# Last two parts of the output: one transfer of 128 partitions each, one on SyncE's and one on ScalarE's queue

## Chip, core and metric

The kernel runs on one core of one Trainium2 chip. The metric is the device time of one execution in microseconds (us). Before the change the median of three runs is 298.77 us (298.04 to 298.97).

## What is computed

Retention attention without softmax, followed by a feed-forward block. The reference, cut to its arithmetic:

```python
# q, k, v: (B, H, S, D) = (8, 8, 576, 64), float32
scores = (1 / sqrt(D)) * q @ k.transpose(0, 1, 3, 2)
gamma = 1.0 - 2.0 ** (-5.0 - arange(H))
Dmat = where(rel >= 0, gamma[:, None, None] ** rel, 0.0)   # rel = position of query - position of key
attn = (scores * Dmat) @ v
x = attn.transpose(0, 2, 1, 3).reshape(4608, 512)
h = x @ w_in                  # w_in: (512, 2048)
g = h * cos(h)
out = g @ w_out               # w_out: (2048, 512); out: (4608, 512) float32
```

## The kernel before

The 4608 tokens are worked through in nine tiles of W = 512 tokens (`NT` = 9, `last` = 8). Attention runs in blocks of 256 tokens ahead of them and leaves `xT`, the bf16 operand of the first matrix product. For each tile, `mm1` (matmuls at line 506) gives `h`, ScalarE gives the cosine (line 519) and VectorE multiplies the two into `gT` (line 522). The second product is `mm2_seven`: the product of a 512-token tile with `w_out` is cut into two by two quarters and made from seven block products instead of eight, numbered 1, 2, 6, 4, 7, 5, 3 in the order in which they run. Each block product covers 256 tokens by `N2` = 256 output columns and 1024 inner elements. The sums of quarters of `gT` that it needs are made at line 565, its matmuls stand in `product` (line 626), ScalarE copies results out of PSUM into `ot` tiles (line 656), and VectorE adds the rest (line 652). The order of the work on every engine is written out by hand; the tile framework adds the semaphore waits that the data need.

A tile of 256 tokens is two groups `j` of P = 128 rows. Within a group, the partition p holds the row 2 * i + r of the group, with r = p // 64 and i = p % 64 (HP = 64): partitions 0 to 63 hold the even rows and partitions 64 to 127 the odd rows. `stored_rows` (line 636; the issues are at line 642) therefore writes a tile by two DMAs of 64 partitions, one for each r, given to the two queues in `queues`:

```python
rows = out[r0 : r0 + P * t.shape[1], c0:c1].rearrange(
    "(j i r) c -> r i j c", r=2, i=HP
)
for r in range(2):
    queues[r].dma_start(rows[r], t[r * HP : (r + 1) * HP])
```

Elsewhere in the kernel both queues are SyncE's; in the last tile, all stores but the first go by one DMA on SyncE's and one on ScalarE's queue.

The place of the change is the very end of the last tile. There the block products 5 and 3 have three parts instead of two, set in `product`:

```python
if x in (5, 3) and n == last:
    parts = [(0, 0, N2), (1, 0, N2 // 2), (1, N2 // 2, N2)]
```

Each part is a group j and a range of columns: 128 rows by 256 columns, then twice 128 rows by 128 columns. Product 3 runs part after part. In the last branch of `mm2_seven`, each part is added to `u1` by VectorE and stored at once, so that the first part's store goes out while TensorE works on the next part.

Of the kernel before, what the change touches and what calls it, by code (L numbers as in the profile page):

```python
# [17 lines left out]
def kernel(  # L18
# [9 lines left out]
    nc = tc.nc  # L28
    P = 128
# [13 lines left out]
    N2 = DM // 2  # L43

    W = 512
# [47 lines left out]
    tiles = {}  # L93
# [496 lines left out]
    def late_sums(n, xs):  # L590
        for x in xs:
            g_sum(n, x, 6 if x == 5 and n > 1 else 0 if x == 3 and n == 2 else 4, E2)
# [43 lines left out]
    def stored_rows(r0, c0, c1, t, queues=(nc.sync, nc.sync)):  # L636
# [7 lines that stand above are left out]
    def mm2_seven(n, at, stored, xs=(1, 2, 6, 4, 7, 5, 3), halfway=None):  # L644
        pend = []

        def flush():
            while pend:
                pend.pop(0)()

        def add(out_, in0, in1):
            return lambda: nc.vector.tensor_tensor(out=out_, in0=in0, in1=in1, op=ALU.add)  # L652

        def copied(tag, x):
            t = op.tile([P, 2, N2], F32, tag=tag, name="ot")
            held.append(lambda ps=tiles["all", x]: nc.scalar.copy(t, ps))  # L656
            return t

        def store(t, r, c, s):
            def go():  # L660
                queues = (nc.sync, nc.scalar) if n == last and s else (nc.sync, nc.sync)
                stored_rows(n * W + r * 256, c * N2, (c + 1) * N2, t, queues)
                stored(s)

            return go

        def copies():
            while held:
                held.pop(0)()

        for x in xs:
            if x not in at:
                copies()
                flush()
            else:
                if at[x].__name__ in ("nothing", "first_scores", "last_outputs", "only_intro", "turning"):
                    copies()
                at[x](flush, pend)
                copies()
            if x == 6 and n > 1:  # L680
                late_sums(n, (3,))
            parts = product(n, x, halfway)
            if x == 1:
                c11 = copied("a", 1)
                tiles["c11"] = c11
                if n > 1:
                    late_sums(n, (5, 6))
            elif x == 2:
                c11 = tiles["c11"]
                if n == 1:  # L690
                    p2 = copied("d", 2)
                    continue
                pend[:0] = [add(c11, c11, tiles["all", 2]), store(c11, 0, 0, 0)]
            elif x == 6:
                u1 = copied("b", 1)
            elif x == 4:
                c21 = copied("c", 4)
            elif x == 7 and n == 1:
                pend += [
                    add(c21, c21, tiles["all", 1]),  # L700
                    add(c22, c22, tiles["all", 1]),
                    store(c21, 1, 0, 1),
                    store(c22, 1, 1, 2),
                    add(c11, c11, p2),
                    store(c11, 0, 0, 0),
                ]
            elif x == 7:
                c22 = copied("d", 1)
                pend += [add(c21, c21, tiles["all", 1]), store(c21, 1, 0, 1)]
            elif x == 5 and n == 1:  # L710
                c22 = copied("d", 5)
            elif x == 5 and n == last:
                for (j, c0, c1), ps in zip(parts, tiles["o", 5]):
                    pend.append(add(c22[:, j, c0:c1], ps, c22[:, j, c0:c1]))
                pend.append(store(c22, 1, 1, 2))
            elif x == 5:
                pend += [
                    add(c22, c22, tiles["all", 5]),
                    add(u1, u1, tiles["all", 5]),
                    store(c22, 1, 1, 2),  # L720
                ]
            elif n < last:
                pend += [add(u1, u1, tiles["all", 5 if n == 1 else 3]), store(u1, 0, 1, 3)]
                flush()
            else:
                flush()
                copies()
                for (j, c0, c1), ps in zip(parts, tiles["o", 5]):
                    add(u1[:, j, c0:c1], ps, u1[:, j, c0:c1])()
                    stored_rows(  # L730
                        n * W + j * P, N2 + c0, N2 + c1, u1[:, j : j + 1, c0:c1],
                        (nc.sync, nc.scalar),
                    )

    loaded, prepared = 2, 0

# [204 lines left out]
    for n in range(NT):  # L941
        blocks = blocks_of.get(n) or [(e + k * E2, 0, W) for e in range(0, E2, 2) for k in range(2)]
        for i, (et, c0, cw) in enumerate(blocks):
# [25 lines left out]
            if (n, i) == (1, 3):  # L969
                mm2_seven(1, {}, None, (1,), lambda: (outputs(3, "m"), off.pop()()))  # L970
# [133 lines left out]
        def stored(u):  # L1104
            if n == 1:
                if u == 0:
                    step(False)
            else:
                steps_to({0: 2 * n + 6, 3: 2 * n + 7}.get(u, 0))

        mm2_seven(n, at, stored, *([(2, 4, 6, 5, 7, 3)] if n == 1 else []))


# [28 lines left out]
```

## Time and profile before

| | |
|---|---|
| median of the runs | 298.77 us (298.04, 298.97, 298.77) |
| profiled execution | 298.03 us |
| its span, first to last instruction | 296.3 us |
| TensorE matmuls busy | 284.4 us, 96% of the span |
| TensorE weight loads busy | 195.9 us, 66% |
| VectorE busy | 215.7 us, 73% |
| ScalarE busy | 170.2 us, 57% |
| GpSimd busy | 141.1 us, 48% |
| granted TensorE clock | 0.997 |
| read from and written to HBM | 36.70 MB and 9.44 MB |

In the profile's names PE is TensorE's matmuls, PEld its weight loads, DVE is VectorE, ACT is ScalarE, POOL is GpSimd and SP is SyncE; a q behind the name (SPq, ACTq) is the engine's sequencer, which among other things issues DMAs. L642 is line 642 of the kernel. Busy shares are averages over the whole span; the chain of waits tells which engine's work the end waited for. An issue's duration is the time for which it holds its queue; the data move later, and the landing is the time from the start of the issue to the last completion.

### The profile page before, as it was taken

What the parts mean: (1) busy time and instruction counts of PE and PEld (TensorE: products, weight loads), DVE (VectorE), ACT (ScalarE), POOL (GpSimd) and SP (SyncE); (2) the same over time, 40 slices, a digit from 0 to 9 for tenths busy, and PEclk for the clock granted to TensorE, in tenths of its full rate; (3) what the DMA queues carried; (4) which work ended last, traced back from release to release, by engine and by line L of the source; (5) the groups of instructions that cost most, each with busy time, mean ns of one, the idle gap of its engine ahead of it and who ended that gap; (6) DMA issues with size and microseconds to landing.
All of it is one profiled execution on the core that took longest, in us unless ns stands there. A gap on an engine that the chain in (4) does not pass through costs nothing.

```text
span 296.3 us, 10512 instructions
## 1 busy us (share of the span) xinstructions
PE 284.4 (96%) x4366; PEld 195.9 (66%) x4386; DVE 215.7 (73%) x307; ACT 170.2 (57%) x200; POOL 141.1 (48%) x162
## 2 busy tenths in 40 slices
PE   7989999889999999999999999999999999999994
PEld 2568545768864687458845884588458845884584
DVE  5756747859947887698769866986698669745943
ACT  4856316467458844767476747684668466535620
POOL 7621454961495995349424952495149013101400
PEclk9999999999999999999999999999999999999998
DMA  7999999988979958833965289429201220112013
GB/s 224 282 207 220 243 242 219 251 217 218 235 177 226 233 122 189 205 83 79 226 156 115 60 211 215 91 48 260 57 0 40 53 57 0 40 44 65 0 38 106
DMA packets 103981, 42.62 MB, mean 144 GB/s; under 512 B 68480, under 2 KB 103424, under 8 KB 103936
## 3 DMA queue, kind: packets, MB, share of 16 engines
q1 hardware_dynamic: 99184, 37.37, 52.0%
q0 software_dynamic: 4224, 4.19, 8.5%
q8 instruction: 36, 0.59, 0.9%
q10 hardware_dynamic: 528, 0.39, 0.4%
q14 instruction: 9, 0.07, 0.1%
HBM read 36.70 MB, written 9.44 MB: 156 GB/s over the span
## 4 chain that ended last, share of the span: by engine, by line
PE 84%; DMA 5%; DVE 4%; ACT 3%; issue 1%; POOL 1%; SPq 1%; ACTq 0%; POOLq 0%
PE h L506 39%; PE o L626 32%; PE o L1012 4%; DMA w_in_sb<-in_moe_w_in_dram 3%; PE tr L238 3%; PE ov L436 2%; DMA fk<-in_k_dram 2%; PE ov L463 1%; PE st L351 1%; PE sc L318 1%; ACT qkT L244 1%; DVE ret L327 1%; DVE gT L522 1%; SPq L139 1%; POOL qks L202 1%
## 5 line engine op out<-in xcount | busy, mean ns | idle before, releaser
L506 PE MATMUL h<-xT,w_in_sb 128*128 128x512 bf16 (+1 forms) x689 | 126.9, 340 | 1.4 <-DVE gT L522 0.2
L522 DVE TENSOR_TENSOR gT<-h,cosh 128x1024 bf16<-128x1024 f32 x72 | 87.6, 1221 | 32.1 <-ACT cosh L519 31.7
L506 PEld LDWEIGHTS <-w_in_sb 128*128 128x128 bf16 x704 | 68.0, 98 | 55.6 <-DMA w_in_sb<-in_moe_w_in_dram 0.7
L519 ACT ACTIVATE cosh<-h,half_pi 128x1024 f32<-128x1024 f32 x72 | 79.9, 1114 | 39.2 <-PE h L506 39.2
L565 POOL TENSOR_TENSOR gs<-gT 128x512 bf16<-128x512 bf16 x28 | 35.8, 1278 | 100.5 <-DVE gT L522 100.3
L626 PEld LDWEIGHTS <-gs 128*128 128x128 bf16 x528 | 49.6, 98 | 6.0
L626 PEld LDWEIGHTS <-gT 128*128 128x128 bf16 x384 | 36.6, 98 | 6.1
L202 POOL TENSOR_TENSOR qks<-fk,gkc 128x512 bf16<-128x512 f32 x32 | 37.6, 1193 | 5.1 <-DMA fk<-in_k_dram 5.1
L652 DVE TENSOR_TENSOR ot<-ot,o 128x512 f32<-128x512 f32 x35 | 23.2, 683 | 22.9 <-ACT ot L656 12.1
L202 POOL TENSOR_TENSOR qks<-fq,gq 128x512 bf16<-128x512 f32 x29 | 32.2, 1129 | 9.8 <-DMA fq<-in_q_dram 9.6
L244 ACT COPY qkT<-tr 128x1024 bf16<-128x1024 bf16 x28 | 26.8, 1021 | 9.9 <-PE tr L238 9.9
L410 ACT CAST sb<-s_all 128x768 bf16<-128x768 f32 (+2 forms) x18 | 16.3, 904 | 25.4 <-DVE s_all L400 21.1
L626 PE MATMUL o<-w_out_sb,gs 128*128 128x256 bf16 (+1 forms) x264 | 30.6, 270 | 0.1
L626 PE MATMUL o<-w_out_sb,gT 128*128 128x256 bf16 x256 | 30.6, 273 | 0.0
L626 PE MATMUL o<-ws,gs 128*128 128x256 bf16 (+1 forms) x264 | 30.4, 269 | 0.0
L656 ACT COPY ot<-o 128x512 f32<-128x512 f32 x33 | 19.2, 583 | 16.1 <-PE o L626 16.1
L327 DVE TENSOR_TENSOR ret<-sc,mask_c 128x512 bf16<-128x512 f32 x32 | 20.7, 684 | 5.9 <-PE sc L318 4.0
L213 POOL CAST vb<-fv 128x512 bf16<-128x512 f32 x32 | 19.9, 645 | 4.2 <-DMA fv<-in_v_dram 4.2
L400 DVE TENSOR_TENSOR s_all<-st,s_all 128x256 f32<-128x256 f32 x49 | 20.7, 422 | 1.2
L482 ACT CAST xT<-ov 128x1024 bf16<-128x1024 f32 x16 | 16.2, 1012 | 9.2 <-PE ov L463 9.1
L565 DVE TENSOR_TENSOR gs<-gT 128x512 bf16<-128x512 bf16 (+1 forms) x25 | 16.7, 667 | 0.5
L626 PE MATMUL o<-ws,gT 128*128 128x256 bf16 x128 | 15.3, 273 | 0.0
(77 smaller groups left out, 208.0 us busy)
## 6 DMA issues: line engine op xcount, KB each, us to landing
out_dram<-ot SPq DMA_DIRECT2D x68, 128.0 KB, 2.5
fk<-in_k_dram SPq DMA_DIRECT2D x28, 256.0 KB, 4.9
fv<-in_v_dram SPq DMA_DIRECT2D x28, 256.0 KB, 4.8
fq<-in_q_dram SPq DMA_DIRECT2D x12, 512.0 KB, 5.2
w_in_sb<-in_moe_w_in_dram POOLq DMA_DIRECT2D x4, 512.0 KB, 8.4
w_out_sb<-in_moe_w_out_dram POOLq DMA_DIRECT2D x4, 512.0 KB, 9.1
fq<-in_q_dram SPq DMA_DIRECT2D x4, 384.0 KB, 5.4
fk<-in_k_dram SPq DMA_DIRECT2D x2, 512.0 KB, 5.0
```

The costliest lines, as they stand in the source:

```text
L202: return eng.tensor_tensor(out=dst.rearrange("p b a d -> p a b d"), in0=src.rearrange("p (a b) d -> p a b d", a=2), in1=by.rearrange("p (a ...
L213: runs[y](vb[:, y], f[:, :, y, :] if j < NP_B else f[:, y])
L244: evacs[r](tiles["qkT", j][:, :, :, :, r * HP : r * HP + HP], pss[r])
L327: nc.vector.tensor_tensor(out=ret[:, he].rearrange("p b y i -> p (b y) i"), in0=ps[he].rearrange("p b y i -> p (b y) i"), in1=mask_c.unsqu ...
L400: nc.vector.tensor_tensor(out=s32[:, u], in0=ps[c.half][:, c.y], in1=s32[:, u - 1] if u else tiles["run"], op=ALU.add,)
L506: nc.tensor.matmul(ps[:, j, :], lhsT=w_in_sb[:, dg, (et + j) * P : (et + j + 1) * P], rhs=xT[:, dg, c0 : c0 + w], start=(dg == 0), stop=(d ...
L519: nc.scalar.activation(cosh, ps, ACTF.Sin, bias=half_pi, scale=1.0)
L522: nc.vector.tensor_mul(gT[:, et : et + m, c0 : c0 + w], ps, cosh)
L565: i = eng.tensor_tensor(out=tiles["gs", n, x][:, e : e + step], in0=a[:, e : e + step], in1=b[:, e : e + step], op=op_,)
L626: nc.tensor.matmul(dst[i], lhsT=lhs[:, e, j * P : (j + 1) * P], rhs=rhs[:, e, c0:c1], start=(fresh and e == 0 and (i == 0 or len(parts) > 2)),
L652: return lambda: nc.vector.tensor_tensor(out=out_, in0=in0, in1=in1, op=ALU.add)
L656: held.append(lambda ps=tiles["all", x]: nc.scalar.copy(t, ps))
```

## The change

In the last branch of `mm2_seven`, the first part is stored as before, by `stored_rows` with two DMAs. The second part goes out by one DMA on SyncE's queue and the third by one DMA on ScalarE's queue. Each of them covers all 128 partitions: its source is `u1[:, j, c0:c1]`, 128 partitions of 128 float32 values (512 bytes), and its destination is the view `(i r) c -> r i c` of the 128 rows. Bytes, values and the order of the adds stay the same.

```diff
             else:
                 flush()
                 copies()
-                for (j, c0, c1), ps in zip(parts, tiles["o", 5]):
+                for (j, c0, c1), ps, whole in zip(parts, tiles["o", 5], (None, nc.sync, nc.scalar)):
                     add(u1[:, j, c0:c1], ps, u1[:, j, c0:c1])()
-                    stored_rows(
-                        n * W + j * P, N2 + c0, N2 + c1, u1[:, j : j + 1, c0:c1],
-                        (nc.sync, nc.scalar),
-                    )
+                    r0, c0, c1, t = n * W + j * P, N2 + c0, N2 + c1, u1[:, j, c0:c1]
+                    if whole is None:
+                        stored_rows(r0, c0, c1, t.unsqueeze(1), (nc.sync, nc.scalar))
+                    else:
+                        whole.dma_start(
+                            out[r0 : r0 + P, c0:c1].rearrange("(i r) c -> r i c", r=2),
+                            t,
+                        )
```

## The prediction

> **What bounds the kernel now.** I read the chain of waits first, because it says which engine's work sets the end, and then the last microseconds, because the change touches only those.
>
> ```profile
> PE 84%; DMA 5%; DVE 4%; ACT 3%; issue 1%; POOL 1%; SPq 1%; ACTq 0%; POOLq 0%
> ```
>
> In the merged chain, in order of time, the last pieces are:
>
> ```profile
> 279.94 12.40 PE o L626 x128
> 292.35 0.02 issue
> 292.37 0.29 DVE ot L652
> ```
>
> TensorE is the bound until 292.35 us. One VectorE add of 0.29 us follows and ends at 292.66. The span ends at 296.29, so 3.63 us are left in which no compute engine works; they belong to the output stores. No instruction of TensorE, VectorE or ScalarE before the last three adds is changed, so everything happens in this tail. The timeline of the two issuing queues (start, duration), restricted to the tail:
>
> ```profile
> 291.93 0.49 SPq L642 DMA_DIRECT2D out_dram<-ot  x1
> 291.94 0.51 ACTq L642 DMA_DIRECT2D out_dram<-ot  x1
> 292.52 0.55 SPq L642 DMA_DIRECT2D out_dram<-ot  x1
> 292.54 0.81 ACTq L642 DMA_DIRECT2D out_dram<-ot  x1
> 293.16 0.56 SPq L642 DMA_DIRECT2D out_dram<-ot  x1
> 293.44 0.56 ACTq L642 DMA_DIRECT2D out_dram<-ot  x1
> ```
>
> These are three parts of two issues each: 64 rows of 1024 bytes, then twice 64 rows of 512 bytes. The last add was done at 292.66, but ScalarE's queue began its last issue only at 293.44, since each issue holds its queue for 0.5 to 0.8 us. That is 0.78 us of queueing on the path. The trace's records of single packets and semaphore writes give the rest: that last issue's first data packet starts at 294.68 (1.24 us after the issue began), its last packet ends at 294.97, its completion arrives at 295.32 (0.35 us later), and from there to the end of the span are 0.98 us of closing waits and barrier.
>
> Next I asked how a transfer uses the 16 DMA engines. From the page's table of queues and its table of DMA issues:
>
> ```profile
> q10 hardware_dynamic: 528, 0.39, 0.4%
> out_dram<-ot ACTq DMA_DIRECT2D x2, 128.0 KB, 2.9
> out_dram<-ot ACTq DMA_DIRECT2D x1, 64.0 KB, 2.4
> out_dram<-ot ACTq DMA_DIRECT2D x2, 32.0 KB, 2.0
> ```
>
> Queue q10 is ScalarE's: its five issues move 2 x 128 + 64 + 2 x 64 = 448 pieces of 1024 or 512 bytes. The 80 packets above that are 5 x 16: each transfer ends with 16 completion writes, one for each DMA engine. So all of these transfers run on 16 engines. In each, the outermost count of both patterns is 64. Finally the price of a packet, from the windows view (columns: stretch, busy us and instructions of each engine, clock, DMA share, GB/s):
>
> ```profile
> 0.00:8.00 8.00, 6.17 (x29) 2.36 (x29) 4.57 (x23) 3.76 (x7) 5.71 (x29) 1.00 0.79 233
> 294.30:294.70 0.40, 0.00 (x0) 0.00 (x0) 0.00 (x0) 0.00 (x0) 0.00 (x0) 0.67 0.32 87
> ```
>
> The first 8 us hold loads made of 512-byte packets alone: 233 GB/s x 8 us / 512 B = 3,641 packets in 0.79 x 16 x 8 = 101 engine-microseconds, or 27.8 ns each, in long streams of 64 packets for each engine and load. The 0.40 us of the last stores: 68 packets in 2.05 engine-us, 30 ns with their completion writes; the records put the stores' packets alone at 28 ns. So one engine takes about 28 ns for 512 bytes in either direction, one packet after another.
>
> **The change, part by part.**
>
> *Issues removed.* Two of the last four go: ScalarE's half of the second part (0.81 us) and SyncE's half of the third (0.56 us). SyncE's issue for the second part stays at 292.52. ScalarE's queue is free at 292.45, so its issue for the third part starts when the add allows, at about 292.70 (the other issues follow their add or their predecessor by 0.03 to 0.10 us), instead of 293.44: 0.74 us earlier. Nothing is queued behind these issues but the closing waits.
>
> *Issues made larger.* 128 rows in place of 64. The earlier stores with 128 pieces hold SyncE for 0.60 us against 0.55, so 0.05 us more. On ScalarE, beside a running SyncE issue, the bounds are 0.56 and 0.81 us: ScalarE's first packet falls between 293.9 and 294.2.
>
> *The pattern.* The source walks 128 partitions. The destination, `(i r) c -> r i c` with r=2, walks 2, then 64, then the columns. No transfer in the trace has an outermost count that 16 does not divide (64, 128, 96 and 32 are the counts there), so none shows how many engines such a one gets. The bounds are 16 (as everywhere) and 2: a transfer that is cut along the outermost count of both patterns can only be cut into parts that both counts, 128 and 2, allow. I take 2, since a cut in 16 would have to run through the second count of one pattern but through the first of the other, and every row here is explained by a cut along the outermost.
>
> The Trainium skill, "DMA: Bandwidth & Descriptors", section "Why a DMA increments its semaphore by 16 and not by 1", states just this: the number of engines is the largest up to 16 that divides the slowest count of both patterns, on the lowest-numbered engines; no run here shows it yet. By it the sum is the one below, with both transfers on one pair. The same page's "Rules for kernel authors" advises one 128-partition transfer instead of two halves; by that alone the sum would be the rival with 16 engines.
>
> *The sum with two engines.* Each transfer puts 64 packets on each of its two engines; the two transfers on the same pair make 128 x 27.8 ns = 3.56 us for each engine. SyncE's first packet comes at 293.74 + 0.05 = 293.79 (its present issue at 292.52 has it 1.22 us later). ScalarE's come before SyncE's 64 are through (293.79 + 1.78 = 295.57), so the pair never runs dry. Data end: 297.35. Completion, +0.35: 297.70. Closing, 0.98, and 0.1 more because the last completion is now that of an earlier semaphore in SyncE's closing list (its waits there follow each other by 0.06 us): 298.78. Against 296.29 that is **+2.5 us**. The profiled execution took 298.03, so it would be 300.5; it is the lowest of the runs shown (298.04 to 298.97, median 298.77), and on the median I forecast **301.3 us**. With packets of 25 ns (the shortest recorded) the added time is 2.1 us, with 33 ns 3.2 us: on the runs from 298.04 to 298.97 this case's own range is 300.1 to 302.2.
>
> **The rivals.**
>
> *Sixteen engines (not slower).* If the hardware cuts along all 128 rows, the earlier issue decides. ScalarE's first packet at 293.9 to 294.2, 8 packets an engine (0.22 us) and 0.18 us by which the engines start one after another: data end at 294.3 to 294.6, where it was 294.97. Less the 0.1 us of closing that is -0.3 to -0.6 us: 298.2 to 298.5 us, about 298.3. For it speaks that every transfer in the trace uses 16; against it that all of those have outermost counts that 16 divides. It decides from about seven engines up: both transfers hold 256 packets, 7.1 engine-microseconds, and must be through by 294.87 (today's 294.97 less the 0.1), 1.08 us after 293.79; 7.1 / 1.08 = 6.6. With 4 engines the end would be 295.6, and the change would already lose.
>
> *Two engines each, but different ones.* Then ScalarE's 64 packets end at about 294.05 + 1.8 = 295.85, 0.9 us after today's end, and with the closing +1.0: 299.7. Against it: all engines serve both queues in the trace, and there is no reason for one queue to begin its cut elsewhere.
>
> *Two engines, slower packets.* The middle of the kernel has 1024-byte store packets of 67 ns, the tail some of 46; at 46 ns a 512-byte packet the term is 5.9 us and the time 303.6, at 67 ns 8.6 and 306.3. A queue that alternates with another on one engine could cost this. Against it: at a DMA share of 0.79 to 0.99, loads keep to 28 to 30 ns.
>
> **How the numbers follow.** Two engines, one pair, 28 ns: 0.70. Sixteen engines: 0.14. Different pairs: 0.07. Slower packets: 0.09. Predicted is the likeliest, 301.3. From 300.1 to 302.2 and the case of different pairs hold a little over 0.75; reaching up to 303.3 takes in the milder slow packets, and down to 298.2 most of the case of 16 engines, so that about 0.1 is left out. What a measurement of this kernel can tell from no change is about 0.3%, 0.9 us. All the two-engine cases but a part of the different pairs are slower by more: 0.84. The 16 engines' -0.3 to -0.6 us lies within it, with a small part beyond: same 0.13, faster 0.03.
>
> **What would show it.** Queue q10 counts it: 448 data packets and 3 x 16 completions in both cases, and 2 more (498) with two engines or 16 more (512) with sixteen; q1 falls by 30 or by 16 from 99184. In windows between 294.6 and 297.2 the DMA share should stand near 2/16 = 0.12, at some 37 GB/s (2 x 512 B / 27.8 ns). The last add should end 3.6 us before the end of the span now and about 6.1 us after the change; all before 292.66 should be as it was. Both 64 KB transfers should land about 5 us after their issue, where the 32 KB ones take 2.0 today. Wrong would be: q10 at 512 and a last landing near 294.8; or 498 with a share that falls below 0.10 (slower packets) or of 0.25 while both run (two pairs).

## The result and the profile after

With the change the kernel takes 301.17 us (median of 13 runs) where it took 298.77 (13 runs beside them): 0.86% slower, ratio 1.0086 with a 95% interval of 1.0063 to 1.0109, or 1.9 to 3.3 us. The forecast was 301.3 us by the case of two DMA engines. Single runs of some kernels are over 1.5% longer than the fastest of the same kernel; the ratios here and below leave these out.

The profiled execution took 302.28 us with a span of 300.6. Its last pieces of the chain of waits:

```profile
281.99 12.40 PE o L626 x128
294.41 0.29 DVE ot L652
```

TensorE's last stretch takes the same 12.40 us, and the add the same 0.29. But the add ends at 294.70, 2.0 us later than in the profile of before, and only the remaining 2.2 us of the longer span lie behind it. What is ahead of the tail differs from execution to execution: over the kernels of this document, which differ there in nothing or almost nothing, the last add ends between 292.7 and 297.2 us. I therefore compare the **tail**, from the end of the last add to the end of the span, each read from one profiled execution. It was 3.63 us before and is 5.86 us now, +2.23 us, inside the 1.9 to 3.3 us of the runs. The kernel that has the same transfers with the queues exchanged (below) shows the two parts separate: its add ends at 293.34 and its tail is 6.17.

The profile page's table of DMA queues (packets, MB moved, share of the 16 engines' span) counts the engines that took part. SyncE's queue q1 before, then q1 and q10 after:

```profile
q1 hardware_dynamic: 99184, 37.37, 52.0%
q1 hardware_dynamic: 99154, 37.37, 51.2%
q10 hardware_dynamic: 498, 0.39, 0.4%
```

498 is 448 packets of data, 16 completions for each of three transfers, and 2 for the whole one; q1 is lower by 30, which is one whole transfer with 2 completions where two halves had 32. Both whole transfers ran on two engines. The timeline has their issues (start, duration):

```profile
294.56 0.61 SPq L734 DMA_DIRECT2D out_dram<-ot  x1
294.73 1.24 ACTq L734 DMA_DIRECT2D out_dram<-ot  x1
```

ScalarE's issue does begin 0.03 us behind the add, as planned, and holds its queue for 1.24 us. In the windows view (columns after the stretch: busy us of PE, PEld, DVE, ACT and POOL; granted clock; DMA share; GB/s) the DMAs are then slow:

```profile
296.00:297.00 1.00, 0.00 (x0) 0.00 (x0) 0.00 (x0) 0.00 (x0) 0.00 (x0) 1.00 0.14 39
297.00:298.00 1.00, 0.00 (x0) 0.00 (x0) 0.00 (x0) 0.00 (x0) 0.00 (x0) 1.00 0.14 43
298.00:299.00 1.00, 0.00 (x0) 0.00 (x0) 0.00 (x0) 0.00 (x0) 0.00 (x0) 0.95 0.14 43
```

At 43 GB/s one of two engines moves 512 bytes in 512 / 21.5 = 23.8 ns; the packet records show starts 23.5 ns apart, each packet recorded as 27 ns long, so neighbours overlap. Two engines out of 16 counted with this overlap make 2 / 16 x 27 / 23.5 = 0.14, the share in these rows. Last, SyncE's closing waits (in total, times, longest), before and after:

```profile
SPq L1137 <- DMA out_dram<-ot: 1.2, 3, 0.5
SPq L1141 <- DMA out_dram<-ot: 4.0, 4, 2.7
```

### The profile page after: what moved, and what is told of

Same layout as the page of the kernel before. It is cut to its first block, busy times and chain, and to the rows that moved or that the text cites. A ratio compares the mean times of both kernels' runs of the same rounds, so it can differ in the third digit from the quotient of the medians.

```text
span 300.6 us, 10528 instructions
## 1 busy us (share of the span) xinstructions
PE 286.5 (95%) x4386; PEld 196.1 (65%) x4386; DVE 216.1 (72%) x307; ACT 170.3 (57%) x200; POOL 141.4 (47%) x162
## 4 chain that ended last, share of the span: by engine, by line
PE 83%; DVE 6%; DMA 4%; ACT 3%; SPq 1%; issue 1%; POOL 0%; ACTq 0%
PE h L506 38%; PE o L626 31%; PE o L1016 5%; DMA fq<-in_q_dram 3%; PE ov L436 3%; PE tr L238 3%; DVE gT L522 2%; PE ov L463 2%; PE st L351 1%; PE sc L318 1%; SPq L139 1%; DMA fv<-in_v_dram 1%; ACT qkT L244 1%; DVE ret L327 1%; ACT cosh L519 1%
```

## Experiments

Theory one: the destination's outermost count decides how many DMA engines a transfer gets, and the packets of two transfers on one pair of engines are the loss. Theory two: a whole transfer of 128 partitions is slow by itself, as ScalarE's issue of 1.24 us suggests. The first four kernels change only the destination's pattern.

### The outermost count

`rows_in_order`, `outer_16`, `outer_8` and `outer_4` each change one line of the changed kernel; with these patterns the rows of the two parts land in another order in `out`:

```diff
-                            out[r0 : r0 + P, c0:c1].rearrange("(i r) c -> r i c", r=2),
+                            out[r0 : r0 + P, c0:c1],                                      # rows_in_order
+                            out[r0 : r0 + P, c0:c1].rearrange("(i r) c -> r i c", r=16),  # outer_16
+                            out[r0 : r0 + P, c0:c1].rearrange("(i r) c -> r i c", r=8),   # outer_8
+                            out[r0 : r0 + P, c0:c1].rearrange("(i r) c -> r i c", r=4),   # outer_4
```

Rows in order:

> The two whole transfers of the change, but partition p goes to row p of its group: the destination's outermost count is 128 instead of 2 (the rows of these two parts land in another order, nothing else differs). 'Tail' is the time from the end of the last VectorE add to the end of the span: 3.63 us before, 5.86 us with the change. Theory one, the outermost count sets the number of DMA engines: 16 engines again, q10 512 packets (448 of data, 4 x 16 completions). ScalarE's issue starts right behind the add instead of 0.78 us later; first packet 1.2 to 1.8 us after that, 0.3 us of packets, 0.35 to the completion, 1.0 to close: tail 2.9 to 3.5 us, time 0.1 to 0.7 us under the kernel before, which a time alone cannot tell from no change. Theory two, a whole 128-partition transfer on one queue costs more by itself (its ScalarE issue took 1.24 us against 0.56 for half of it): tail 5.9 as with the change, 2.2 us slower than before.

Sixteen:

> As the change, with r=16 in place of r=2, so the destination walks 16, then 8 rows (the rows land in another order). Theory one: 16 engines, q10 512, tail 2.9 to 3.5 us. Theory two: 5.9. A third possibility, any two-level destination is slow whatever its counts: 5.9 here while the plain rows are fast.

Eight:

> As the change, with r=8 (the rows land in another order). Theory one: 8 engines, q10 504 packets, 32 packets for each engine over both transfers, at 23.5 to 28 ns 0.75 to 0.9 us; tail 3.0 to 3.7 us, about that of the kernel before (the prediction had the break-even between 6 and 7 engines). Theory two: 5.9.

Four:

> As the change, with r=4 (the rows land in another order). Theory one: 4 engines, q10 500 packets, 64 packets for each engine, 1.5 to 1.8 us from SyncE's first packet 1.1 us after the last add; completion 0.35, closing 1.0: tail 4.0 to 4.3 us, 0.4 to 0.7 us over the kernel before. Theory two: 5.9.

Measured, with the packet and semaphore records giving the data end (from the last add to the last data packet's end):

(Ratios here and below are against runs of the kernel before on the same chip, whose median was 298.7 to 298.9 us. `rows_in_order` has a median below the 298.82 us of its kernel before and a ratio above 1: three of its twelve runs took 300.3 to 301.4 us, which move the ratio but hardly the median.)

| outermost count | q10 packets | data end, us | tail, us | median, us | ratio (95% interval) |
|---|---|---|---|---|---|
| 64, in halves (before) | 528 | 2.31 | 3.63 | 298.77 | 1 |
| 128 (rows_in_order) | 512 | 1.77 | 3.14 | 298.39 | 1.0007 (0.9981 to 1.0034) |
| 16 | 512 | 1.76 | 3.15 | 298.26 | 0.9979 (0.9965 to 0.9993) |
| 8 | 504 | 2.14 | 3.53 | 298.62 | 0.9994 (0.9981 to 1.0007) |
| 4 | 500 | 2.95 | 4.31 | 299.34 | 1.0041 (1.0012 to 1.0070) |
| 2 (the change) | 498 | 4.49 | 5.86 | 301.17 | 1.0086 (1.0063 to 1.0109) |

Every tail is where theory one put it, at worst 0.01 us beyond. Theory two wanted 5.9 in all rows and falls; so does the thought that a destination of two levels is slow in itself, since 16 x 8 is as quick as plain rows. The completions say outright how many engines worked: 448 and 48 taken off leave 16, 16, 8 and 4. q10 with the counts 16, 8 and 4:

```profile
q10 hardware_dynamic: 512, 0.39, 0.4%
```

```profile
q10 hardware_dynamic: 504, 0.39, 0.4%
```

```profile
q10 hardware_dynamic: 500, 0.39, 0.4%
```

In the windows view of the kernel with count 4, while both transfers run, the share is about 4 / 16 and the rate nearly twice that of two engines:

```profile
298.40:299.20 0.80, 0.00 (x0) 0.00 (x0) 0.00 (x0) 0.00 (x0) 0.00 (x0) 1.00 0.27 79
```

The break-even, which the prediction put between 6 and 7 engines, lies between 4 (slower than before by 0.68 us of tail) and 8 (quicker by 0.10).

ScalarE's issue tells a second thing. With 16 engines (`rows_in_order`) and with 8:

```profile
293.01 0.65 ACTq L734 DMA_DIRECT2D out_dram<-ot  x1
```

```profile
293.35 1.32 ACTq L734 DMA_DIRECT2D out_dram<-ot  x1
```

It took 0.65 us for both 16-engine patterns and 1.32, 1.26 and 1.24 us for 8, 4 and 2 engines; SyncE's took 0.54 to 0.70 throughout.

### Which transfer, which queue

These keep r=2 and change who sends what; the tuple names the queue of a whole transfer for each part, `None` for two halves.

```diff
-                for (j, c0, c1), ps, whole in zip(parts, tiles["o", 5], (None, nc.sync, nc.scalar)):
+                ... (None, nc.sync, nc.sync)):    # both_on_sync
+                ... (None, None, nc.scalar)):     # third_alone, third_again
+                ... (None, nc.sync, None)):       # second_alone
+                ... (None, nc.scalar, nc.sync)):  # swapped
```

> As the change (r=2), but both whole transfers on SyncE's queue. Theory one: the pair of DMA engines is what the end waits for, whichever queue feeds it: 128 packets for each of the two engines at 23.5 to 28 ns from 1.1 us after the last add, tail 5.5 to 6.0 us, q10 480 less what ScalarE no longer moves (2 x 128 + 64 of data and 3 x 16 completions, 368). A rival within it: two queues that alternate on one engine are what makes it slow; then one queue alone would end earlier, below 5.3 us. If ScalarE's issue of 1.24 us with the change came from two queues issuing at once, SyncE's second issue here should take 0.6 us; if it comes from a transfer on two engines right behind another, it should be long here too.

Measured: tail 5.94 us, 301.21 us (four runs), ratio 1.0081 (1.0057 to 1.0106), q10 368 packets. One queue alone is no better than two, so the alternation of queues on an engine is not the cost, and the queues do not have pairs of their own: with pairs of their own, ScalarE's 64 packets of 23.5 ns would have ended 3.3 us after the add in the change (first packet at 1.84), and one queue for both would have cost 1.2 us more, where it cost 0.1. SyncE's second issue took 0.52 us, so a long issue is not what a two-engine transfer always brings.

> Only the third part is one whole transfer (r=2, on ScalarE); the second goes as before in halves on both queues. Theory one: ScalarE's queue is held by its half of the second part until about 0.7 us after the last add, as before; then the issue, first packet 2.0 to 2.6 us after the add, 64 packets on each of two engines at 23.5 to 28 ns, 1.5 to 1.8 us; completion 0.35, closing 1.0: tail 4.8 to 5.7 us, q10 514 packets. So half of the packets on the pair, but little of the loss gone, since the third part starts late again.

Measured: tail 4.89 us, at the near end of what was expected. The count of 514 was wrong arithmetic of mine: ScalarE's queue also carries its half of the second part, so it is 512 of data and 4 x 16 + 2, and 578 is what the page has. ScalarE's issue took 1.08 us here, with no SyncE issue under way. The ratio came out at 1.0102 (1.0060 to 1.0144), more than a tail longer by 1.26 us explains, so it was run once more:

> The kernel with only the third part whole (r=2, on ScalarE), once more with more rounds: its tail was 4.89 us, 1.26 over the kernel before, or 0.42% of the time, while its ratio came out at 1.0102 (1.006 to 1.0144). If the tail is all that differs, the ratio falls to about 1.004; if something ahead of the tail is later with this kernel, it stays at 1.006 or more.

Measured: 300.23 us, ratio 1.0035 (0.9999 to 1.0070), tail 4.90. The first ratio came from four runs that scattered from 299.93 to 303.74; the tail was the same to 0.01 us both times. The second ratio is near the 1.004 of the tail alone, but its interval does not exclude 1.006.

> Only the second part is one whole transfer (r=2, on SyncE); the third goes as before in halves on both queues. Theory one: the pair of engines takes 64 packets each from 1.1 us after the last add, 1.5 to 1.8 us, and about 8 of the third part's packets each among them (0.2 us): data end 2.8 to 3.1 us after the add, completion 0.35, closing 1.0: tail 4.1 to 4.5 us, 0.5 to 0.9 us over the kernel before.

Measured: tail 4.48 us, 299.71 us, ratio 1.0050 (1.0023 to 1.0077). So either transfer alone on the pair already costs more than the earlier issue gives back: +0.85 us for the second part, +1.26 for the third, +2.23 for both.

> As the change (r=2), with the queues exchanged: the second part on ScalarE, the third on SyncE. One pair of DMA engines as the bound: the same 128 packets an engine from 1.1 to 1.3 us after the last add, tail 5.7 to 6.0 us. ScalarE's issue held its queue for 1.24 us with the change, 1.26 and 1.32 with four and eight engines, 0.65 with sixteen, SyncE's 0.5 to 0.7 always. If that belongs to ScalarE's queue on fewer than 16 engines, it is 1.1 us or more here too though it comes first; if it belongs to the later of the two issues, SyncE's is the long one here.

Measured: tail 6.17 us, 301.17 us, ratio 1.0083 (1.0053 to 1.0114). The timeline:

```profile
293.21 1.16 ACTq L734 DMA_DIRECT2D out_dram<-ot  x1
293.36 0.60 SPq L734 DMA_DIRECT2D out_dram<-ot  x1
```

The long issue stays with ScalarE although it comes first: it belongs to that queue on fewer than 16 engines. The tail misses the expectation by 0.2 us. From the first packet to the last the two transfers took 3.59 us, where they took 3.38 with the change. In part that is because the two engines finished further apart, by the last completions 0.41 us instead of 0.23, so that in the last stretch the rate falls from 42 to 28 GB/s; the rest is open:

```profile
296.40:297.40 1.00, 0.00 (x0) 0.00 (x0) 0.00 (x0) 0.00 (x0) 0.00 (x0) 0.92 0.14 42
297.40:298.20 0.80, 0.00 (x0) 0.00 (x0) 0.00 (x0) 0.00 (x0) 0.00 (x0) 0.50 0.09 28
```

### A version with whole transfers on 16 engines

Rows can only be plain if partition p holds row p. In `ordered`, the last tile's multiply writes its columns in the order of the rows, and all stores of that tile are plain, two of them on ScalarE's queue and the others on SyncE's (the diff is cut):

```diff
+                by = [t.rearrange("p m (u r i) -> p m u r i", u=4, r=2) for t in (ps, cosh)]
+                nc.vector.tensor_mul(
+                    gT[:, et : et + m, :].rearrange("p m (u i r) -> p m u r i", u=4, r=2), *by
+                )
...
-                for (j, c0, c1), ps in zip(parts, tiles["o", 5]):
+                for (j, c0, c1), ps, whole in zip(parts, tiles["o", 5], (nc.sync, nc.scalar, nc.sync)):
...
+                    whole.dma_start(out[r0 : r0 + P, c0:c1], t)
```

> A version that keeps one transfer for each part and 16 engines: in the last tile VectorE writes gT with its columns in the order of the rows (position 2*i + r instead of 64*r + i), so that partition p holds row p; every store of the last tile is then one plain transfer of 128 partitions, outermost count 128; the three last go on SyncE, ScalarE and SyncE. Theory one: SyncE's last issue begins 0.03 us after the last add, takes 0.6 us, first packet at 1.25, 0.4 us of packets, completion 0.35, closing 1.0: tail 3.0 to 3.2 us against 3.63 before, if the 8 multiplies with a strided write keep their 1.22 us. Time about 0.5 us below the kernel before (ratio about 0.998). Theory two (whole transfers cost more by themselves): no better than before.

Measured: 297.95 us against 298.66, ratio 0.9980 (0.9963 to 0.9997); tail 2.85 us, 0.78 us less than before. It is the quickest of the kernels here whose output has its rows in place, by 0.2%, a gain that the interval only just separates from none. The condition set on it was missed: the multiplies took 1.31 us instead of 1.22. The last issues in its timeline are short:

```profile
293.11 0.35 ACTq L744 DMA_DIRECT2D out_dram<-ot  x1
293.56 0.35 SPq L744 DMA_DIRECT2D out_dram<-ot  x1
```

The last one starts 0.03 us behind the add, its packets 0.85 us later, and the data end at 1.22 us after the add. The closing took 1.29 us instead of 0.98. SyncE ends the program with nine waits in a fixed order of semaphores, and when nothing is left to wait for they still follow each other by 0.06 us. Here the last landing is on the semaphore of the third wait, with six more behind it; before it was that of the eighth, with one behind it, and 5 x 0.06 us make the difference. In the other kernels the closing is 1.03 to 1.04 us where two waits are left and 0.97 to 0.98 where one is.

## Why the prediction was right

**Two engines.** The step on which all hung, a cut along the outermost counts of both patterns, is shown: 498 packets, and the series 16, 8, 4, 2. The Trainium skill, "DMA: Bandwidth & Descriptors", section "Why a DMA increments its semaphore by 16 and not by 1", has this as its rule for the number of engines, and the traces agree, with 16, 8, 4 and 2 completions for the counts 16, 8, 4 and 2. Which two engines of the 16 they are no run here shows; that both transfers have the same pair, `both_on_sync` shows. The Trainium skill's advice in "DMA: Bandwidth & Descriptors", section "Rules for kernel authors", one 128-partition transfer rather than two halves, holds here only where the outermost count is large enough: the tail is 3.14 us with 128 and 3.53 with 8, 4.31 with 4 and 5.86 with 2, against 3.63 for the halves.

**The sum, in us from the end of the last add:**

| term | predicted | measured |
|---|---|---|
| SyncE's first packet | 1.12 | 1.10 |
| 128 packets on each engine | 3.56 | 3.38 |
| last packet to completion | 0.35 | 0.33 |
| closing | 1.08 | 1.04 |
| tail | 6.11 | 5.86 |

The mechanism was right and the one term noticeably off is the packets: I took the recorded length, 27.8 ns, for the spacing, which is 23.5 ns once both engines run evenly. It was not the full 128 x 4.3 ns = 0.55 us less: among the first few packets of the two engines some are recorded at up to 66 ns, and three later ones at 51 to 74 ns. Why these are slower is open. That the median came within 0.13 us of the forecast is in part luck: the tail grew by 2.23 us where the sum had 2.48, and the medians differ by 2.40, since what runs ahead of the tail scatters.

**The earlier issue.** ScalarE's issue began 0.75 us earlier, as forecast with 0.74. Its length, bounded at 0.81 us, was 1.24: the bound came from 16-engine transfers. So ScalarE's first packet came 1.84 us behind the add, outside the predicted 1.24 to 1.54. It cost nothing with two engines, since SyncE's packets kept the pair busy until then.

**The rivals.** Sixteen engines with -0.3 to -0.6 us is what `rows_in_order` and `outer_16` gave, -0.49 and -0.48 us of tail: the price was right, the condition was not met. Different pairs are excluded by `both_on_sync`, slower packets by the 23.5 ns.

**What should be seen.** q10 at 498 and q1 lower by 30 were exact; the share is 0.14 and the rate 39 to 43 GB/s where I had 0.12 and 37, the same mis-sized packet. The landings came 4.5 and 4.8 us after the issues where I had 5. One sign did not show: all before the last add should have been as it was, and in the profile the add ended 2.0 us later; executions scatter there by more than that.

## What to carry to other kernels

Before joining transfers, write down the outermost count of both patterns as the instruction walks them: a rearranged destination whose first count is 2 left 14 of the 16 DMA engines idle although the source has 128 partitions, and the completions in the profile page's queue table show it at once. At the end of a program, where nothing covers a transfer, one issue less on each queue was worth about 0.5 us here, but only where the joined transfer kept all engines; putting the data in the order of the rows ahead of the store gets both. Where the part of a kernel ahead of the change scatters by more than the effect, compare the tail from the last compute instruction to the end of the span.

## What the runs showed that I had not expected

An issue on ScalarE's queue for a transfer on fewer than 16 engines held the queue for 1.08 to 1.32 us in six profiles, with SyncE issuing beside it or not, and 0.65 us for 16 engines in the place of the change; SyncE's took 0.52 to 0.70 us there for any count. Why is not settled. It sets the end where the engines would be done early: with eight engines ScalarE's first packet came 1.61 us after the add, against 1.24 and 1.36 with sixteen.

A plain 128-partition store issued while the other queue was idle, or all but idle, held its queue for 0.35 us (`ordered`), less than a 64-partition half (0.49 to 0.60 us on SyncE before). Most of that is not the neighbour: in the kernel before, 58 halves went out on SyncE with no issue on another queue beside them and held it for 0.60 us in the median, 128 pieces of 1024 bytes each, while the plain stores with 256 such pieces in `ordered` took 0.38 to 0.43 us, alone as well. With the other queue issuing beside it, the plain form took 0.54 and 0.65 us (`rows_in_order`), so the neighbour counts too; the two were not varied separately in one place.
